# Retention followed by a low-rank mixer and MLP: loads in the order of need, positional decay, tiled low-rank steps, and the next batch's retention woven by hand into the MLP

## The chip, the cores and the metric

One core of one Trainium2 chip. The metric is the time of one execution on the device, in microseconds (us), lower is better. A run more than 1.5% above the fastest of the same kernel is called slow, and slow runs are left out of every comparison. The granted clock is the share of its full rate at which TensorE may run, by the profile's record, as a mean over the run.

Words used throughout: "up" is the first matmul of the MLP and "down" the second; a "tile" or "piece" is one sum in one bank of PSUM, TensorE's output memory; to "evict" is to copy a sum out of its bank, after which the bank is free; qd and kd are q and k with the decay multiplied in, vb is v cast to bfloat16.

Engines in the profile: PE is TensorE's matmuls, PEld its weight loads, DVE is VectorE, ACT is ScalarE, POOL is GpSimd, SP is SyncE, which issues loads and stores.

## The reference

Batch 4, 8 heads, 768 tokens, head size 64, model width 512. First a retention with a decay for each head, then a mixer over tokens of rank 32, then an MLP of width 2048 over channels:

```python
gamma = 1.0 - 2.0 ** (-5.0 - np.arange(H))            # per head
for t in range(S):
    state = gamma * state + outer(k[t], v[t])         # per batch and head, 64 x 64
    y[t]  = scale * q[t] @ state
x  = y as (batch, tokens, heads*head_dim)             # 768 x 512
h  = x.T @ U @ V                                      # U 768 x 32, V 32 x 768
u  = x + h.T
out = u + relu(u @ w_ch1) @ w_ch2                     # 512 -> 2048 -> 512
```

Inputs and output are float32; both kernels multiply in bfloat16.

## The kernel before

Tokens go in six chunks of 128. Retention of a chunk is done with matmuls: scores of the chunk against itself under a mask that holds the decay, plus the query times the state carried from the chunk before.

```python
def retnet_chunk(b, ci, x_sb, state_sb):
    # three loads of 256 KB: q_n, k_n, v_n (ring of three buffers each)
    nc.gpsimd.tensor_tensor(qd, q_n, Gq, op=ALU.mult)     # decay by place in the chunk
    nc.gpsimd.tensor_tensor(kd, k_n, Gk, op=ALU.mult)
    nc.scalar.activation(vb, v_n, AF.Copy)
    # ... 8 matmuls against the identity: qT_p, kT_p; two ACT evictions
    # ... 8 score matmuls with 64 rows; two DVE multiplies by maskA, maskB
    # ... o_p = a @ vb (+ qT @ state); one ACT eviction into x_sb[:, ci]
    for p in range(4):
        nc.tensor.matmul(st_p[:, ts(p, P)], kd[:, ds(2 * p, 2)], vb[:, ds(2 * p, 2)],
                         start=True, stop=first)
        if not first:                                     # the old state, decayed by gI
            nc.tensor.matmul(st_p[:, ts(p, P)], gI[:, ts(p, P)], state_sb[:, ts(p, P)],
                             start=False, stop=True)
    nc.vector.tensor_tensor(ns, st_p, bmask, op=ALU.mult)
```

The mixer of a batch is a list of tasks: a projection with 32 stationary columns, eight pieces of uT, 32 up pieces, six down tiles. Sums take turns in two PSUM banks, 6 and 7:

```python
def t_proj():
    for j in range(NCK):                                  # 6 matmuls of 512 columns
        nc.tensor.matmul(p_p, Ub[:, j], x_sb[:, j], ...)
def t_uT(c, lo, sz, idx):
    nc.tensor.matmul(piece, P_sb[:, ts(c, P)], Vb[:, ds(lo, sz)], ...)    # 32 rows
    # ... plus x transposed through the identity; evicted by ACT or DVE in turn
def t_mlp1(m, lo, sz):
    g_p = bank(6 + m % 2, free=sz)                        # 4 matmuls, then ReLU
def t_mlp2(j):
    nc.tensor.matmul(ch_p, Vb[:, ds(j * P, P)], P_sb, start=True, stop=False)
    # ... 16 matmuls of 512 columns; DVE adds x; store
```

The order of the whole:

```python
retnet(0)
retnet(1)
setup_weights()                                           # 8.4 MB, on ScalarE's queue
interleave(mixer_tasks(0, xs[0]), 2)                      # mixing of 0 with retention of 2
interleave(mixer_tasks(1, xs[1]), 3)
for t in mixer_tasks(2, xs[2]): t()
for t in mixer_tasks(3, xs[3]): t()
```

A scheduler at build time fixes the order of instructions on each engine. Each engine has its own list: in the run a_uv_late below, a ScalarE instruction that waited 5.00 us for its load held up the one behind it, which needed nothing from it.

## Time and profile before

| | kernel before |
|---|---|
| timed, two runs | 323.53 and 330.51 us |
| profiled span | 321.5 us |
| first low-rank matmul of batches 0 to 3 (PE timeline) | 75.2, 137.8, 200.2, 260.0 us |
| first up matmul of batches 0 to 3 | 84.2, 147.9, 210.3, 267.5 us |

The page of the profile, kernel before: the span cut into 40 slices of 8 us. Digits are tenths of busy time; PEclk is the granted TensorE clock in tenths; GB/s is what the DMA engines moved.

```profile
span 321.5 us, 4612 instructions
...
PE   0246845768999999999999999899999988999995
...
PEclk9999975555999999999999999759999995999999
DMA  7999999999994533154000011000001110000111
GB/s 240 251 291 261 258 245 308 213 277 217 159 189 100 129 99 99 65 148 82 2 2 2 35 65 65 35 0 0 0 2 65 65 67 0 0 0 2 65 65 65
```

PE is full or nearly so (8 or 9) from the tenth slice to the last but one, and DMA before that. There are two lower stretches of PEclk after the start, near 205 to 215 us and at 265 us. The table of stretches of the kernel before, cut where the mixing of a batch begins (start:end, length, busy time of each engine with its instructions, then clock, DMA share and GB/s):

```profile
core 0: us, PE busy (x) PEld busy (x) DVE busy (x) ACT busy (x) POOL busy (x), PEclk, DMA share, GB/s
0.00:75.20 75.20, 39.05 (x400) 29.34 (x400) 39.18 (x80) 35.40 (x68) 34.35 (x32) 0.80 1.13 258
75.20:137.80 62.60, 61.61 (x443) 32.38 (x448) 24.91 (x43) 21.99 (x43) 15.18 (x12) 0.97 0.59 127
137.80:200.20 62.40, 61.50 (x465) 33.00 (x469) 26.06 (x45) 21.61 (x43) 12.52 (x10) 1.00 0.19 51
200.20:260.00 59.80, 56.39 (x287) 26.12 (x290) 16.89 (x29) 11.48 (x23) 0.00 (x0) 0.91 0.07 27
260.00:321.50 61.50, 54.22 (x265) 25.07 (x268) 16.67 (x28) 9.80 (x20) 0.00 (x0) 0.94 0.08 30
```

The first 75 us move 258 GB/s. (The DMA share adds up the time of packets and can pass 1.) Each later line is one batch of mixing; the first two hold the retention of another batch as well. The last two do not, but for one last chunk, yet are only 1 to 3 us shorter: they also have the lower clock.

The chain of work that ended last, kernel before, over the loading stretch (start, length, what):

```profile
0.74 6.18 DMA q_n<-in_q_dram
...
17.00 10.44 DMA k_n<-in_k_dram
...
34.44 7.57 DMA k_n<-in_k_dram
...
42.84 14.58 DMA q_n<-in_q_dram x2
...
62.52 6.86 DMA st<-in_moe_w_ch_dram
...
75.28 2.69 PE bk_71_942 L228 x6
```

The chain goes from load to load, and reaches the first mixing matmul at 75.28 us. Last, the PE timeline of the kernel before, where batch 2 does its up pieces of 256 columns (start, length, line, output, operands):

```profile
229.50 0.60 PE L259 MATMUL bk_263_2608<-uT_2435,w1b 128*128 128x256 bf16 x4
229.93 0.60 PE L259 MATMUL bk_264_2614<-uT_2435,w1b 128*128 128x256 bf16 x4
230.61 0.60 PE L259 MATMUL bk_265_2620<-uT_2435,w1b 128*128 128x256 bf16 x4
```

The starts are 0.43 and 0.68 us apart in turn, so 1.1 us a pair. Four matmuls of 256 columns would be 0.43 us, by the 0.216 us measured for one of 512: every second piece waits for one of two banks to be evicted.

### The profile page before, as it was taken

To read this page: it belongs to the slowest core of one execution; us is meant where nothing else is said; L and a number is where in the kernel's file an instruction comes from. 1 tells how busy PE (TensorE), PEld (TensorE's weight loads), DVE (VectorE), ACT (ScalarE), POOL (GpSimd) and SP (SyncE) were. 2 spreads that over 40 slices of the span, in tenths; PEclk is the share of its full clock that TensorE was granted. 3 is DMA by queue.
4 is the path that set the end of the run, shared out by engine and by line. 5 is a ranking of instruction groups with operands and counts; after the bars stand their busy time and mean duration, and the time that the engine had idled before them with its cause. 6 is when DMAs were issued, how large, how long until landed. Compare 5 with 4: busy or idle time off the path is not lost.

```text
span 321.5 us, 4612 instructions
## 1 busy us (share of the span) xinstructions
PE 272.8 (85%) x1852; PEld 145.9 (45%) x1872; DVE 123.7 (38%) x222; ACT 100.3 (31%) x197; POOL 62.0 (19%) x54
## 2 busy tenths in 40 slices
PE   0246845768999999999999999899999988999995
PEld 0135734544546744455467444334554433455441
DVE  4864534354555531155456121424322122342111
ACT  2436653643655510055454000313310011322000
POOL 0556552637314310063041000000000000000000
PEclk9999975555999999999999999759999995999999
DMA  7999999999994533154000011000001110000111
GB/s 240 251 291 261 258 245 308 213 277 217 159 189 100 129 99 99 65 148 82 2 2 2 35 65 65 35 0 0 0 2 65 65 67 0 0 0 2 65 65 65
DMA packets 83412, 34.04 MB, mean 106 GB/s; under 512 B 76192, under 2 KB 76192, under 8 KB 83392
## 3 DMA queue, kind: packets, MB, share of 16 engines
q1 hardware_dynamic: 79168, 25.37, 36.5%
q10 hardware_dynamic: 4224, 8.39, 7.6%
q8 instruction: 14, 0.23, 0.3%
q14 instruction: 6, 0.05, 0.1%
HBM read 27.46 MB, written 6.29 MB: 105 GB/s over the span
## 4 chain that ended last, share of the span: by engine, by line
PE 71%; DMA 14%; DVE 5%; issue 4%; POOL 3%; ACT 1%; SPq 1%; POOLq 0%; DVEq 0%
DMA q_n<-in_q_dram 6%; DMA k_n<-in_k_dram 6%; DMA st<-in_moe_w_ch_dram 2%; POOL kd L165 2%; POOL qd L164 2%; DVE gT_2436 L265 1%; DVE gT_2813 L265 1%; PE bk_328_3168 L278 1%; PE bk_327_3147 L278 1%; PE bk_325_3105 L278 1%; PE bk_324_3084 L278 1%; PE bk_281_2791 L278 1%; PE bk_278_2728 L278 1%; PE bk_277_2707 L278 1%; PE bk_228_2339 L278 1%
## 5 line engine op out<-in xcount | busy, mean ns | idle before, releaser
L259 PEld LDWEIGHTS <-w1b 128*128 128x128 bf16 x512 | 49.6, 100 | 41.4 <-issue 15.0
L164 POOL TENSOR_TENSOR qd<-q_n,Gq 128x512 bf16<-128x512 f32 x24 | 31.4, 1307 | 87.2 <-PE bk_149_1646 L173 24.3
L165 POOL TENSOR_TENSOR kd<-k_n,Gk 128x512 bf16<-128x512 f32 x24 | 30.8, 1285 | 20.7 <-DMA k_n<-in_k_dram 8.1
L171 PEld LDWEIGHTS <-qd 128*128 128x128 bf16 x96 | 9.3, 116 | 19.9 <-POOL qd L164 16.1
L166 ACT ACTIVATE vb<-v_n 128x512 bf16<-128x512 f32 x24 | 15.0, 627 | 9.6 <-DMA v_n<-in_v_dram 5.1
L278 PEld LDWEIGHTS <-gT_2436 128*128 128x128 bf16 x96 | 8.9, 98 | 11.3 <-issue 1.4
L278 PEld LDWEIGHTS <-gT_940 128*128 128x128 bf16 x96 | 8.9, 98 | 11.2 <-issue 1.4
L278 PEld LDWEIGHTS <-gT_1688 128*128 128x128 bf16 x96 | 8.9, 98 | 11.2 <-issue 1.4
L278 PEld LDWEIGHTS <-gT_2813 128*128 128x128 bf16 x96 | 8.9, 98 | 11.3 <-issue 1.4
L173 PEld LDWEIGHTS <-kd 128*128 128x128 bf16 x96 | 8.7, 113 | 11.0 <-POOL kd L165 9.6
L198 PEld LDWEIGHTS <-aA 128*128 128x128 bf16 x96 | 10.3, 110 | 6.8 <-DVE aA L191 5.8
L198 PEld LDWEIGHTS <-aB 128*128 128x128 bf16 x96 | 10.6, 114 | 4.2 <-DVE aB L192 3.5
L171 PE MATMUL bk_1_176<-ident,qd 128*128 128x128 bf16 x4 | 0.8, 308 | 13.2 <-POOL qd L164 13.2
L210 PEld LDWEIGHTS <-kd 128*128 128x128 bf16 x80 | 9.0, 118 | 4.0 <-issue 3.8
L187 PEld LDWEIGHTS <-kT 64*128 64x128 bf16 x192 | 7.7, 108 | 6.2 <-ACT kT L178 3.2
L213 PEld LDWEIGHTS <-gI 128*128 128x128 bf16 x64 | 7.5, 119 | 4.7 <-issue 4.2
L202 PEld LDWEIGHTS <-qT 128*128 128x128 bf16 x80 | 8.8, 110 | 0.3
L244 ACT ACTIVATE uT_2812<-bk_283_2823 128x512 bf16<-128x512 f32 x1 | 0.6, 597 | 26.4 <-PE bk_283_2823 L241 26.4
L177 ACT ACTIVATE qT<-bk_230_2393 128x512 bf16<-128x512 f32 x1 | 0.6, 597 | 22.5 <-PE bk_231_2394 L173 22.5
L177 ACT ACTIVATE qT<-bk_148_1645 128x512 bf16<-128x512 f32 x1 | 0.6, 597 | 22.0 <-PE bk_149_1646 L173 22.0
L275 PEld LDWEIGHTS <-Vb 32*128 32x128 bf16 x24 | 2.2, 91 | 9.2 <-issue 8.9
L132 ACT ACTIVATE w1b<-st 128x2048 bf16<-128x2048 f32 x2 | 3.8, 1906 | 4.0 <-DMA st<-in_moe_w_ch_dram 4.0
(801 smaller groups left out, 593.2 us busy)
## 6 DMA issues: line engine op xcount, KB each, us to landing
st<-in_moe_w_ch_dram ACTq DMA_DIRECT2D x8, 1024.0 KB, 6.7
q_n<-in_q_dram SPq DMA_DIRECT2D x24, 256.0 KB, 5.1
k_n<-in_k_dram SPq DMA_DIRECT2D x24, 256.0 KB, 4.9
v_n<-in_v_dram SPq DMA_DIRECT2D x24, 256.0 KB, 4.9
out_dram<-o_sb SPq DMA_DIRECT2D x24, 256.0 KB, 2.0
Uf<-in_moe_U_dram SPq DMA_DIRECT2D x1, 96.0 KB, 7.1
Vf<-in_moe_V_dram SPq DMA_DIRECT2D x1, 96.0 KB, 6.4
```

The source lines that it names most:

```text
L164: nc.gpsimd.tensor_tensor(qd, q_n, Gq, op=ALU.mult)
L165: nc.gpsimd.tensor_tensor(kd, k_n, Gk, op=ALU.mult)
L166: nc.scalar.activation(vb, v_n, AF.Copy)
L171: nc.tensor.matmul(qT_p[:, ts(p, P)], qd[:, ds(2 * p, 2)], ident, start=True, stop=True)
L173: nc.tensor.matmul(kT_p[:, ts(p, P)], kd[:, ds(2 * p, 2)], ident, start=True, stop=True)
L187: nc.tensor.matmul(sp[:, ts(h // 2, P)], hsl(kT, h), hsl(qT, h), start=True, stop=True)
L198: nc.tensor.matmul(o_p[:, ts(h, D)], a[:, ts(h // 2, P)], vb[:, h], start=(h % 2 == 0), stop=(first and h % 2 == 1))
L202: nc.tensor.matmul(o_p[:, ts(p, P)], qT[:, ts(p, P)], state_sb[:, ts(p, P)], start=False, stop=True)
L210: nc.tensor.matmul(st_p[:, ts(p, P)], kd[:, ds(2 * p, 2)], vb[:, ds(2 * p, 2)], start=True, stop=first)
L213: nc.tensor.matmul(st_p[:, ts(p, P)], gI[:, ts(p, P)], state_sb[:, ts(p, P)], start=False, stop=True)
L259: nc.tensor.matmul(g_p, w1b[:, c, ts(m, P)], uT_sb[:, c, ds(lo, sz)], start=(c == 0), stop=(c == NCB - 1))
L278: nc.tensor.matmul(ch_p, gT_sb[:, m, ds(j * P, P)], w2b[:, m], start=False, stop=(m == NM - 1))
```

## The change

The intent is to start the MLP sooner and to give PE less to do and fewer waits. The kernel is rewritten; its core, shortened and in places paraphrased:

```diff
-    rin: q_n, k_n, v_n, three buffers each; weights through their own staging on ScalarE's queue
+    RING = 30                        # one FIFO of 256 KB loads on one queue, in the order of use:
+    for ci in range(NCK): feed_chunk(0, ci)          # batch 0
+    ... w1 (16 loads), w2 (16 loads) ...
+    for b in range(1, B): ...                        # batches 1 to 3
@@ decay by place in the whole sequence: the state needs no decay of its own
-        nc.gpsimd.tensor_tensor(qd, q_n, Gq, op=ALU.mult)
+        nc.gpsimd.tensor_tensor(qd, q_n, gq[:, ci, :, None].to_broadcast([P, H, D]), op=ALU.mult)
-            nc.tensor.matmul(st_p[...], gI[...], state_sb[...], start=False, stop=True)
+            # st_p stays in its bank; each chunk adds to it
@@ q and k transposed into one bf16 bank, evicted at once by DVE
-        nc.scalar.activation(qT, qT_p, AF.Copy); nc.scalar.activation(kT, kT_p, AF.Copy)
+        nc.vector.tensor_copy(out=qkT, in_=tp.rearrange("p (n m) -> p n m", n=8))
@@ low rank in tiles of the array
-                nc.tensor.matmul(p_p, Ub[:, j], x_sb[:, j], ...)                   # 512 columns
+                nc.tensor.matmul(p_p[ds(RK * c, RK), :P], Ub[:, j], x_sb[:, j, ts(c, P)], ...)
+                nc.tensor.matmul(banks[c - c0][...], V4[ds(RK * c, RK), ts(j, P)], pc[ds(RK * c, RK)], ...)
+        # u = x + low rank is formed (DVE), kept, and transposed for the MLP
@@ MLP
-                g_p = bank(6 + m % 2, free=sz)
+                g_p = bank("mlp", bufs=3)
-                nc.tensor.matmul(ch_p, Vb[:, ds(j * P, P)], P_sb, start=True, stop=False)
-                nc.vector.tensor_tensor(o_sb, ch_p, x_sb[:, j], op=ALU.add)
+                nc.vector.tensor_tensor(o_sb, ch, u[:, j], op=ALU.add)
@@ order by hand on PE, GpSimd and SyncE
-    retnet(0); retnet(1); setup_weights(); interleave(...)
+    with tc.manual_schedule(engines={ENG.PE, ENG.Pool, ENG.SP}):
+        load_uv()
+        for s in retnet_steps(0): s()
+        ... casts of w1 and w2 ...
+        for b in range(1, B):
+            if b == 1:
+                for s in lowrank_steps(0): s()
+            weave(mlp_pieces(b - 1), retnet_steps(b) + lowrank_steps(b),
+                  0.5 if b == 1 else 0.02, 0.97)
+        for _, f in mlp_pieces(B - 1): f()
```

The steps of retention are turn(c) (transposes and state), score(c) and mix(c), issued as turn(c+1), score(c), mix(c). ScalarE and VectorE are still ordered by the scheduler. One thing more changes: of three up pieces ScalarE now evicts two and VectorE one, where they took turns before.

## The prediction

> **What bounds it now.** The profiled span is 321.5 us (timed 323.5 to 330.5). In the PE timeline, mixing of batch 0 starts at 75.2 us, of 1 at 137.8, of 2 at 200.2, of 3 at 260.0. Two regimes:
>
> - 0 to 75 us: loading. The DMA row stands near 9 at 258 GB/s, and the chain of waits runs through q_n, k_n and weight loads: retention of two batches (9.4 MB) and all weights (8.4 MB) come before the first mixing. PE's clock is half from 50 to 80 us, and before 37 us 128-column matmuls also start 107 ns apart.
> - 75 to 321 us: PE, 88 to 98% busy. Four 512-column matmuls start 0.86 us apart (216 ns each); the Trainium skill ("TensorE: Matmul & The Clock Gate", Back-to-back issue gap) gives 512/2.4 + 2.5, the same. Counting columns, one batch of mixing is 110,592 (46 us), one of retention 19,456 (8 us). Batches 0 and 1 take 62.5 us each against 54; 2 and 3 about 60 against 46: two dips to half clock (205 to 215 and near 265 us, in the sparse low-rank stretch) and the two-bank wait of the 256-column up matmuls (1.1 us a pair, not 0.87).
>
> **Costing.**
>
> 1. Loads in need order: only batch 0 (4.7 MB) stands before the weights. In the trace, stretches with q/k/v alone move about 220 GB/s, weights about 330. Estimate: batch 0 landed at 26 us, w1 at 40, w2 at 53. Retention of batch 0 ends at 37; its low-rank part is a bare chain (projection, four expands on two banks, three turns on one) at 0.69 us per 512-column DVE eviction, about 1.2 for 1,024: 11 us. First up matmul at 48 us, not 84. Retention of batch 1 moves into batch 0's MLP; its PE time returns there.
> 2. PE columns: no Vb matmul in down (-3,072), column-tiled projection (-2,300 if four tiles run together), row-tiled expand (-1,500), no gI matmuls (-2,048): mixing 103,700, retention 17,408. About 15 us in all.
> 3. Three MLP banks: about 3 us a batch.
> 4. Low-rank steps spread between MLP pieces: the dips go, 8 to 10 us.
> 5. Given back: DVE takes per chunk the qkT eviction (1.2), state and two masks (2.1), then expand adds and turns: about 30 us a batch. For batch 1, woven into half an MLP, DVE is near full and each mix waits for masks issued one 0.75 us step earlier: 6 to 8 us of stalls. Batches 2 and 3 have 1.5 us per step: 2 to 3 each. The Trainium skill ("TensorEngine Tiling (Array Packing)", PSUM Bottleneck) warns that tiling speeds TensorE, not eviction.
>
> **Sum.** 48 + 2.5 (cold clock at MLP start) + 4 x 41.8 (MLP) + 3 x 7.7 (retention) + 3 x 3 (low rank) + 12 (stalls) + 3.7 (tail) = 265. Some 35 of the saving come from the earlier start.
>
> **Predicted: 264 us, 248 to 286.** Faster by over 2%: 0.96; within: 0.02; slower: 0.02.
>
> **Right or wrong by.** First up matmul at 44 to 54 us; up pieces 0.87 and 0.44 us apart; down tile 3.5; no clock dip after 55 us; batch-to-batch 52 to 56 us; DVE 75% and more from 70 to 100 us; four projection tiles per 55 to 60 ns.
>
> **What would make it wrong.** Casts, ordered on ACT and DVE by a scheduler I don't see, could hold batch 0's evictions until w2 lands (+5 to 15). The clock may dip in the weaves (+5 to 15). Tiled matmuls may serialise (+2 to 6). A shorter low-rank chain or fewer stalls would give 250.

## The result, and the profile after

The changed kernel ran in 275.54 and 275.89 us (median 275.72; before 323.53 and 330.51). The ratio is 0.8524, with a 95% interval of 0.8486 to 0.8562. A ratio here is the mean time of one kernel's fast runs over that of the other's fast runs of the same rounds, so not quite the ratio of the medians quoted.

The same rows of the page, changed kernel (slices of 6.8 us):

```profile
span 273.8 us, 4712 instructions
...
PE   0275754799988989978999999999999999999994
...
PEclk9999999999999999999999999999999999999999
DMA  8999999999999999200920211100001111000211
GB/s 155 214 218 226 300 387 383 264 223 218 210 221 219 217 234 248 61 0 38 208 62 4 77 41 77 41 0 2 0 2 62 56 77 38 2 0 0 79 77 77
```

PE is full or nearly so from about 52 us, not 75. No slice shows a lower clock. The first slices must be read with care: the record of the clock holds no entry before 55.4 us, and the row then shows 9 although the matmuls start 107 ns apart for 128 columns, which is half of 2.4 GHz. The Trainium skill ("TensorE: Matmul & The Clock Gate", What's actually happening) names half clock as the idle state, and the spacing agrees. Go by spacing where a row could be a default.

The table of stretches, changed kernel, cut at the first up matmul of each batch and at the last matmul:

```profile
core 0: us, PE busy (x) PEld busy (x) DVE busy (x) ACT busy (x) POOL busy (x), PEclk, DMA share, GB/s
0.00:52.00 52.00, 24.91 (x257) 18.15 (x258) 24.81 (x57) 15.04 (x27) 14.14 (x21) 1.00 1.13 271
52.00:113.90 61.90, 57.84 (x482) 31.73 (x481) 33.55 (x55) 22.53 (x44) 18.96 (x18) 1.00 1.10 210
113.90:172.80 58.90, 55.39 (x482) 31.25 (x481) 30.10 (x51) 17.65 (x35) 12.25 (x12) 1.00 0.22 63
172.80:228.10 55.30, 54.42 (x482) 31.02 (x481) 29.60 (x50) 16.28 (x32) 6.13 (x6) 1.00 0.08 30
228.10:269.80 41.70, 41.67 (x225) 21.80 (x223) 9.72 (x16) 10.67 (x22) 0.00 (x0) 1.00 0.10 39
```

The prediction's sum can be set beside these five lines and the tail:

| term | predicted us | measured us |
|---|---|---|
| first up matmul | 48 | 52.0 |
| batch 0's MLP with batch 1's retention and low rank (2.5 + 41.8 + 7.7 + 3 + 7 of stalls) | 62 | 61.9 |
| batch 1's, with batch 2 (41.8 + 7.7 + 3 + 2.5) | 55 | 58.9 |
| batch 2's, with batch 3 | 55 | 55.3 |
| batch 3's MLP | 41.8 | 41.7 |
| tail | 3.7 | 4.0 |
| sum: span | 265.5 | 273.8 |
| timed less span | not counted | 1.9 |

Two terms hold nearly all of the miss: the start (4.0) and batch 1 (3.9). The up pieces of 256 columns, PE timeline of the changed kernel:

```profile
242.34 0.60 PE L319 MATMUL mlp_2993<-uT_2717,w1b 128*128 128x256 bf16 x4
242.77 0.60 PE L319 MATMUL mlp_2999<-uT_2717,w1b 128*128 128x256 bf16 x4
```

They are 0.43 us apart and no longer come in uneven pairs. In the last batch a down tile takes 3.45 us (16 matmuls).

Where the start goes: the chain of work that ended last, changed kernel, in one chunk of batch 0's retention.

```profile
18.30 0.60 ACT x_183 L240
18.90 0.53 ACT vb_2_269 L179
...
19.46 0.60 PE st_207 L201 x4
...
20.09 0.60 DVE state_2_294 L207
...
20.70 0.68 DVE a_0_1_297 L225
21.38 0.61 DVE a_0_1_299 L225
...
22.03 0.24 PE o_310 L233
...
23.05 0.02 ACT x_183 L240
...
23.54 0.63 ACT vb_3_326 L179
```

This is a loop. The eviction of x comes first on ACT, then the cast of the v after next, then the state matmul, the state on DVE, the two masks, the mix, and the eviction of x again. It takes 4.75 us a chunk (from 18.30 to the next x at 23.05), while the loads of a chunk come every 3.6 us. By the trace (issue of each part's last load, plus its time to landing) batch 0 is in by 27.1 us, w1 by 40.3 and w2 by 51.7, near the predicted 26, 40 and 53; retention still ends at 39.9 us, where the prediction had 37. The low-rank chain after it takes 12.1 us, where it had 11. So of the 4.0 us of the start 2.9 are retention and 1.1 the chain.

Where batch 1 loses: the timeline of all engines, changed kernel, when its up stage begins.

```profile
113.92 1.03 PE L319 MATMUL mlp_1459<-uT_1320,w1b 128*128 128x512 bf16 x4
...
117.34 1.02 PE L319 MATMUL mlp_1502<-uT_1320,w1b 128*128 128x512 bf16 x4 [0.69 <-ACT gT_1458 L326]
...
120.85 1.02 PE L319 MATMUL mlp_1543<-uT_1320,w1b 128*128 128x512 bf16 x4 [0.69 <-ACT gT_1458 L326]
...
124.23 0.68 DVE L347 TENSOR_TENSOR o_4_1397<-mlp_1348,u_613 128x512 f32<-128x512 f32 x1
...
128.77 0.68 DVE L347 TENSOR_TENSOR o_5_1455<-mlp_1418,u_613 128x512 f32<-128x512 f32 x1
```

Up pieces of 512 columns start 1.7 to 1.8 us apart in place of 0.86. After every second one 0.7 us goes to a step of retention; the others wait for the eviction of the piece just before them (0.69 us), as if there were one bank and not three. The last two lines say why: the additions of batch 0's output tiles 4 and 5 come at 124.2 and 128.8 us, though their sums were complete near 108 and 114 us, and each holds a bank of the three until then. VectorE shows no idle time just before either addition, and stood idle for 1.7 to 2.4 us four times from 110 to 122 us: the additions were not kept from it by its load, but came late in its list.

### The profile page after: what moved, and what is told of

It reads as the page before. It is cut to its first block, busy times and chain, and to the rows that moved or that the text cites. A ratio compares the mean times of both kernels' runs of the same rounds, so it can differ in the third digit from the quotient of the medians.

```text
span 273.8 us, 4712 instructions
## 1 busy us (share of the span) xinstructions
PE 234.2 (86%) x1920; PEld 134.0 (49%) x1920; DVE 128.5 (47%) x230; ACT 82.2 (30%) x159; POOL 51.5 (19%) x57
## 4 chain that ended last, share of the span: by engine, by line
PE 75%; DVE 12%; issue 4%; ACT 3%; DMA 3%; ACTq 1%; POOL 1%; DVEq 0%; POOLq 0%
DMA Vf<-in_moe_V_dram 2%; DVE u_613 L284 2%; PE mlp_2001 L342 1%; PE mlp_2711 L342 1%; PE mlp_1905 L342 1%; PE mlp_2820 L342 1%; PE mlp_2110 L342 1%; PE mlp_2615 L342 1%; PE mlp_3183 L342 1%; PE mlp_3143 L342 1%; PE mlp_3083 L342 1%; PE mlp_3163 L342 1%; PE mlp_3123 L342 1%; PE mlp_3103 L342 1%; PE mlp_2772 L342 1%
## 5 line engine op out<-in xcount | busy, mean ns | idle before, releaser
L342 PEld LDWEIGHTS <-gT_2890 128*128 128x128 bf16 x96 | 9.4, 98 | 11.1
L342 PEld LDWEIGHTS <-gT_2180 128*128 128x128 bf16 x96 | 8.6, 98 | 9.0
L342 PEld LDWEIGHTS <-gT_1458 128*128 128x128 bf16 x96 | 8.6, 98 | 9.0
L342 PEld LDWEIGHTS <-gT_712 128*128 128x128 bf16 x96 | 8.0, 98 | 7.0
L188 PE MATMUL qk_196<-ident,qd_0_184 128*128 128x128 bf16 x4 | 0.6, 308 | 11.5 <-POOL qd_0_184 L175 11.5
L279 PEld LDWEIGHTS <-V_80 32*128 32x128 bf16 x96 | 3.6, 97 | 12.0 <-issue 12.0
L175 POOL TENSOR_TENSOR qd_0_911<-in_524,gq 128x512 bf16<-128x512 f32 x1 | 1.3, 1295 | 25.6 <-DMA in_524<-in_q_dram 25.6
L175 POOL TENSOR_TENSOR qd_3_2388<-in_1226,gq 128x512 bf16<-128x512 f32 x1 | 1.0, 1042 | 26.6 <-PE qk_2194 L188 26.6
L188 PEld LDWEIGHTS <-qd_0_184 128*128 128x128 bf16 x4 | 0.3, 130 | 11.5 <-POOL qd_0_184 L175 11.5
L300 ACT ACTIVATE uT_2717<-qk_2850 128x1024 bf16<-128x1024 bf16 x1 | 1.0, 1023 | 14.0 <-PE qk_2850 L295 14.0
L300 ACT ACTIVATE uT_2007<-qk_2140 128x1024 bf16<-128x1024 bf16 x1 | 1.0, 1023 | 13.5 <-PE qk_2140 L295 13.5
L175 POOL TENSOR_TENSOR qd_3_1678<-in_605,gq 128x512 bf16<-128x512 f32 x1 | 1.0, 1042 | 17.5 <-PE qk_1478 L188 17.5
L342 PE MATMUL mlp_1348<-w2b,gT_712 128*128 128x512 bf16 x16 | 4.1, 382 | 0.0
L342 PE MATMUL mlp_1243<-w2b,gT_712 128*128 128x512 bf16 x16 | 4.1, 380 | 0.0
L342 PE MATMUL mlp_1038<-w2b,gT_712 128*128 128x512 bf16 x16 | 4.1, 380 | 0.0
L342 PE MATMUL mlp_905<-w2b,gT_712 128*128 128x512 bf16 x16 | 4.1, 380 | 0.0
L342 PE MATMUL mlp_1143<-w2b,gT_712 128*128 128x512 bf16 x16 | 4.1, 380 | 0.0
L342 PE MATMUL mlp_2001<-w2b,gT_1458 128*128 128x512 bf16 x16 | 4.0, 380 | 0.0
L342 PE MATMUL mlp_2062<-w2b,gT_1458 128*128 128x512 bf16 x16 | 4.0, 380 | 0.0
L342 PE MATMUL mlp_2711<-w2b,gT_2180 128*128 128x512 bf16 x16 | 4.0, 380 | 0.0
```

The lines of the kernel that those rows point to most:

```text
L175: nc.gpsimd.tensor_tensor(qd, q_n, gq[:, ci, :, None].to_broadcast([P, H, D]), op=ALU.mult)
L188: nc.tensor.transpose(tp[:, ts(p, P)], qd[:, ds(2 * p, 2)], ident)
L279: nc.tensor.matmul(banks[c - c0][:, ts(j - j0, P)], V4[ds(RK * c, RK), ts(j, P)], pc[ds(RK * c, RK)], start=True, stop=True)
L300: nc.scalar.activation(dst, src, AF.Copy)
L342: nc.tensor.matmul(ch, gT[:, m, ts(j, P)], w2b[:, m], start=(m == 0), stop=(m == NM - 1))
```

## The experiments

Twelve runs; all gave correct results. All were timed in rounds beside the kernel before except one look. In the four calls (the result's own and three of experiments) the fast runs of the kernel before average between 323.5 and 324.5 us, so differences of about 1 us between kernels of different calls are not read from the times alone. The median leaves out the slow run of b_need_order. "Changed" is 275.7 us.

| run | what | us, median | ratio to before | first up matmul, us |
|---|---|---|---|---|
| b_need_order | before, with the new batch order | 310.1 | 0.9576 | 59.4 (from b_need_order_2) |
| a_two_first | changed, with the old batch order | 283.6 | 0.8755 | 79.1 |
| a_two_banks | changed, two MLP banks | 283.8 | 0.8762 | 52.1 |
| a_bare_lowrank | changed, low rank not woven | 296.4 | 0.9152 | 52.7 |
| a_out6 | changed, six output buffers | 272.0 | 0.8387 | 52.3 |
| a_uv_late | changed, casts of U and V later | 275.3 | 0.8480 | 52.7 |
| a_first_qd | the same, first cast of v off ScalarE | 274.4 | 0.8460 | 50.4 |
| a_deep | changed, retention one step deeper | 263.2 | 0.8115 | 46.5 |
| a_hi_late | changed, part of low rank later | 272.7 | 0.8402 | 49.0 |
| a_best | a_deep, a_hi_late and a_out6 together | 261.5 | 0.8063 | 44.2 |
| a_best30 | a_best, weave from 0.3 | 260.3 | 0.8036 | 43.4 |

### Where the gain comes from: one part alone, three parts undone

Theory: the order of loads is the main source. Rival: the columns, banks and weaving are.

**b_need_order**, the kernel before with one edit:

```diff
-    retnet(0); retnet(1); setup_weights()
-    interleave(mixer_tasks(0, xs[0]), 2); interleave(mixer_tasks(1, xs[1]), 3); mixer 2; mixer 3
+    retnet(0); setup_weights()
+    interleave(mixer_tasks(0, xs[0]), 1); interleave(mixer_tasks(1, xs[1]), 2)
+    interleave(mixer_tasks(2, xs[2]), 3); mixer 3
```

> The kernel before with one thing changed: retention of batch 1 is no longer done ahead of the weights, but interleaved with mixing of batch 0 (2 with 1, 3 with 2). Theory 1 (order of loads and of batches is the main source of the gain): first mixing at 45 to 52 us in place of 75, less some 10 us for retention that is now done later, so a span near 305 us (298 to 310). Rival (the gain is in columns, banks and weaving; the order only moves work about): within 2% of before, 315 us or more.

Three fast runs: 309.21, 310.13 and 311.01 us, 4.2% less than before, some 14 us; their spans, 307.4 to 309.2 us, lie in the theory's range for the span, and the times below the rival's. The fourth run, the profiled one, took 446 us: its record grants a clock of 0.5 to 0.65 from 37 us to the end. Nothing is read from it.

**b_need_order_2**, the same kernel, one look for a usable profile:

> The same kernel as b_need_order, for a profile in the fast state (the first one fell at a granted clock of 0.60). Fast runs gave 309 to 311 us. Expected: first mixing at 45 to 52 us in place of 75.2, batch 0's step longer than 62.5 us by 0 to 3, batch 2's step near 62 in place of 59.8, so that of 25 us of earlier start some 14 are left.

310.89 us, one run, within the range of the fast ones. The projection begins at 39.3 us (45 to 52 was expected), the first up matmul comes at 59.4 in place of 84.2, so 25 us earlier. From projection to projection the batches then take 78, 63 and 63 us. Of 25 us, 14 are left at the end, as expected. The expected step of batch 0 was wrong (78, not 62 to 65): its projection is issued as chunks of x come, and the up stage begins 20 us after it.

**a_two_first**, the changed kernel with the order undone:

```diff
-    for ci in range(NCK): feed_chunk(0, ci)
+    for b in range(2):
+        for ci in range(NCK): feed_chunk(b, ci)
     ... weights ...
-    for b in range(1, B): ...
+    for b in range(2, B): ...
-        for s in retnet_steps(0): s()
+        for s in retnet_steps(0): s()
+        for s in retnet_steps(1): s()
-            rs = retnet_steps(b)
+            rs = retnet_steps(b) if b > 1 else []
```

> The changed kernel with that order undone: loads and retention of batches 0 and 1 both come before the weights and the first mixing. Theory 1: first up matmul near 80 us in place of 52 (a second latency-bound retention of 29 us, and 21 us of loads), batch 0's MLP shorter by 12 to 15 us since no retention is woven into it, so 289 to 294 us, 13 to 18 above the changed kernel. Rival: 275 to 280 us.

283.58 us, 7.9 more than changed; less than expected and more than the rival. The first up matmul comes 27.1 us later (79.1), but batch 0's MLP is 15.3 us shorter (46.6 us, since it carries no retention), and batch 1's 3.6 us shorter (55.3, like batch 2's: the late additions are gone). So a first matmul that is 27 us earlier is worth 8 us in this kernel: what was taken out of the start comes back inside the MLP. The 8 are a low figure: 3.6 us of what the undoing costs are hidden by the late additions going; without them it would be about 11.5, by subtraction, which no run tested.

**a_two_banks**: `bank("mlp", bufs=3)` becomes `bufs=2`.

> The changed kernel with two banks in place of three for the MLP's sums. Theory (the prediction: third bank worth about 3 us a batch): 10 to 14 us more than the changed kernel, 286 to 290 us; up pieces of 256 columns back to 1.1 us a pair. More, up to 20, if late output additions hold both banks. Rival (evictions keep up with two): under 3 us.

283.78 us, 8.1 more, so about 2 us a batch on average where the prediction had 3. Both the theory and the rival were off; the theory by less. In batch 3, where nothing is woven in, the up stage takes 23.3 us in place of 20.9, with pieces of 256 columns about 1.1 us a pair, as in the theory. The average hides a spread: by the first up matmuls the four batches take 3.9, −0.4, 2.1 and 2.3 us more. Batch 1 takes no more because its third bank is of little use in the changed kernel, where late additions hold two of the three. VectorE's order changes with the edit too (those additions come at 117.0 and 120.6 us here), so this run isn't the bank alone.

**a_bare_lowrank**:

```diff
-            weave(mlp_pieces(b - 1), rs + ls, 0.5 if b == 1 else 0.02, 0.97)
+            weave(mlp_pieces(b - 1), rs, 0.5 if b == 1 else 0.02, 0.97)
+            for s in ls: s()
```

> The changed kernel with the eight low-rank steps of batches 1 to 3 done in one piece after the MLP of the batch before, not woven into it; retention stays woven. Theory: each bare chain costs 8 to 10 us in place of about 3 of matmuls, and the clock may drop to half for 7 to 10 us after it as in the kernel before: 12 to 30 us more than the changed kernel. Rival (weaving low rank hides little): under 6 us, and no dip of the clock.

296.37 us, 20.7 more: the largest single part found. The clock row of its page, and the beginning and end of one bare chain in its PE timeline, with the first up pieces after it:

```profile
PEclk9999999999999995799999995899999985999999
```

```profile
107.98 0.52 PE L266 MATMUL o<-x,Ub 128*32 128x128 bf16 x24
...
117.89 1.01 PE L295 MATMUL qk<-ident,u 128*128 128x128 bf16 x8 [1.11 <-ACT uT L300]
...
119.55 1.06 PE L319 MATMUL mlp<-uT,w1b 128*128 128x512 bf16 x2 [0.22 <-issue]
```

The chain takes 10.7 us (107.98 to 118.69) for some 3 us of matmuls at full clock. In the record the clock is at half from 111.7 to 121.9 us, and so twice more, 10.2 us each. The last two lines show it: eight transposes of 128 columns take 1.01 us (0.61 at full clock, in the changed kernel), and the two up matmuls last 1.06 us where two take 0.59 at full clock. No wait of PE within the chain is over 1.11 us; in the 3.7 us from the chain's start to the drop PE was busy for 1.5. So low rank done in one piece costs its own latency and a clock drop that goes on into the MLP. The three undone parts add to 36.7 of the 48 us; the fewer matmul columns (15 us by count) were not undone by themselves, and parts need not add.

### Where the prediction lost 11 us

**a_out6**: `tc.tile_pool(name="outp", bufs=3)` becomes `bufs=6`.

> The changed kernel with six output buffers in place of three. In the changed kernel's trace the up stage of batch 1 starts its first 512-column pieces 1.7 us apart until 129 us, because the additions of output tiles 4 and 5 of batch 0 come at 124.2 and 128.8 us in the vector engine's order, though their sums were complete near 108 and 114, and hold two of the three banks; this order follows from output buffers that are given back late (the stores of tiles 0 and 1 are issued 10 us after they are ready, behind loads in the same queue). Theory: with six buffers the additions come at once, up of batch 1 takes 28 us in place of 31, as in batch 2, and the whole 3 to 5 us less: 271 to 273 us. Rival (the vector engine is simply full there, whatever the order): within 1 us of 275.7.

272.03 us, 3.7 less, as the theory had it. The two additions, VectorE timeline of this run:

```profile
107.86 0.69 DVE L347 TENSOR_TENSOR o<-mlp,u 128x512 f32<-128x512 f32 x1 [0.18 <-PE mlp L342]
...
113.95 0.69 DVE L347 TENSOR_TENSOR o<-mlp,u 128x512 f32<-128x512 f32 x1 [1.03 <-PE mlp L342]
```

They come 16 and 15 us earlier, each as soon as its sum is there. Batch 1's up stage takes 27.7 us in place of 31.2. With three buffers the fifth addition could not have a buffer before the store of tile 1, which sits in the SyncE list behind loads (issued at 99.3 us, ready at 89.8). But in the changed kernel's trace that store had landed 4.8 us after its issue, near 104 us, before the fifth sum was complete, and the store of tile 2 (issued at 103.8, landed 4.1 us later) before the sixth. So what held these additions in the run was their place in VectorE's list and not a buffer. The edit made the scheduler choose another order; that it had reckoned with late buffers is the likely reason, but isn't shown.

**a_uv_late**:

```diff
-        load_uv()                                 # with both casts on GpSimd at once
-        for s in retnet_steps(0): s()
+        uv_casts = load_uv()                      # loads only
+        for i, s in enumerate(retnet_steps(0)):
+            if i == 13: uv_casts()
+            s()
```

> The changed kernel with the two GpSimd casts of U and V moved from ahead of the first chunk to just ahead of the sixth. The first qd comes at 10.4 us since GpSimd waits for V until 9.3. Theory (retention of batch 0 is a chain of latencies, 4.75 us a chunk, that starts with the first qd): first qd at 5.5 to 6.5 us, first up matmul at 47.5 to 48.5 in place of 52.0, 271 to 272 us in all. Rival (the loads of batch 0 set the end of that retention): first up above 50.5, less than 1.5 us gained.

275.32 us: nothing gained, and the first qd came at 10.73 us, later than before the edit (10.42). The timeline of this run shows a second thing that had stood at the same place:

```profile
9.67 0.63 ACT L181 ACTIVATE vb<-in 128x512 bf16<-128x512 f32 x1 [5.00 <-DMA in<-in_v_dram]
10.20 0.23 ACT L142 ACTIVATE gq<-pos 128x48 f32<-128x48 f32 x1
...
10.73 1.04 POOL L177 TENSOR_TENSOR qd<-in,gq 128x512 bf16<-128x512 f32 x1 [9.43 <-DVE gq L144]
```

GpSimd waits for gq, the decay, and ScalarE computes gq only after the cast of the first v, which waits for its load until 9.67 us. An order on ScalarE that no data requires held the first step. This run could not test the theory, since it did not bring about the earlier qd.

**a_first_qd**: a_uv_late, and for the first chunk of batch 0 the cast of v is done by GpSimd:

```diff
-            nc.scalar.activation(vb, v_n, AF.Copy)
+            if b == 0 and ci == 0: nc.gpsimd.tensor_copy(out=vb, in_=v_n)
+            else: nc.scalar.activation(vb, v_n, AF.Copy)
```

> Second try at the start. In a_uv_late the first qd did not come earlier (10.7 us), since the cast of the first v, which waits for its load until 9.7, stands ahead of the two exponentials of the decay in ScalarE's order. Here that one cast is done on GpSimd after the first kd, so the exponentials are first on ScalarE. Theory: gq is ready near 6 us, first qd at 5.5 to 6.5, second turn near 12 in place of 13.9, and with the chunk period of 4.75 us unchanged the first up matmul 1.5 to 2.5 us earlier, total 273 to 274.3. Rival (the loads alone pace batch 0): total within 0.7 of 275.5.

274.38 us. Now the first qd is at 5.25 us, but the second waits for its load until 10.52, and the first up matmul comes 1.6 us earlier (50.4). So of 5 us at the first step 1.6 are left; the loads hold the second chunk. The first up matmul is as the theory had it; the time is 0.1 above its range. It is 0.9 us under a_uv_late: too little to be read from the times. It was run at another time.

**a_deep**:

```diff
-        for ci in range(NCK + 1):      # turn(ci), score(ci - 1), mix(ci - 1)
+        for ci in range(NCK + 2):      # turn(ci), score(ci - 1), mix(ci - 2)
-    rmid = ctx.enter_context(tc.tile_pool(name="rmid", bufs=3))
+    rmid = ctx.enter_context(tc.tile_pool(name="rmid", bufs=4))
```

> The changed kernel with retention pipelined one step deeper: mix of chunk c comes after turn of c+2 and score of c+1, and there are four buffers in place of three. The wait of each mix for its two masks (1.0 and 0.36 us a chunk in batch 0, 0.5 to 0.9 in batch 1) should go. Theory (these waits are on the critical path, as the prediction has it with 6 to 8 us for batch 1): chunk period of batch 0 from 4.75 to about 3.6 us, first up 5 to 7 us earlier, batch 0's MLP 3 to 5 us shorter, in all 8 to 12 us less: 264 to 268 us. Rival (the vector engine's load, or the cast of v behind the x copy, sets the pace): under 3 us.

263.24 us, 12.5 less: slightly more than expected, and the largest gain of a single edit. The casts of v of chunks 2, 3 and 4 of batch 0, ScalarE timeline of this run:

```profile
16.38 0.63 ACT L179 ACTIVATE vb<-in 128x512 bf16<-128x512 f32 x1 [2.98 <-DMA in<-in_v_dram]
...
20.00 0.63 ACT L179 ACTIVATE vb<-in 128x512 bf16<-128x512 f32 x1 [0.61 <-DMA in<-in_v_dram]
...
23.67 0.63 ACT L179 ACTIVATE vb<-in 128x512 bf16<-128x512 f32 x1 [1.09 <-DMA in<-in_v_dram]
```

The period is 3.6 to 3.7 us, and each cast now waits for its load; in the changed kernel these casts stood behind the eviction of x, 4.75 us apart (18.79, 23.54 and 28.29 us in its ScalarE timeline). The first up matmul comes at 46.5 (5.5 earlier), batch 0's step takes 57.6 us in place of 61.9, batch 1's 56.6 in place of 58.9. VectorE does the same work as before the edit (22.8 us in the woven half of batch 0's step in both), so its load was not the bound. PE's recorded waits for the masks of batch 1's mixes, 2.8 us in all in the changed kernel, no longer appear. Some 2 us of the gain are in batch 1's step, where the additions come less late (the sixth 13 us after the first up matmul, not 15; the fifth 3 us after it, not 10).

The edit changes two things at once, and the list of ScalarE with it: three casts of v, not two, now stand ahead of the first eviction of x. So the expected rival's second half, the cast of v behind the x copy, is not ruled out: this edit removes it too. How much each contributes was not separated. A third suspect is the clock, since the record grants full clock from 18.7 to 28.9 us here. But a_best30 below, with the same retention steps for batch 0, has full clock for 3.4 us only (from 19.3) and begins its projection at the same 34.7 us (39.9 in the changed kernel), so the clock is not where the earlier start comes from.

**a_hi_late**:

```diff
-                for s in lowrank_steps(0): s()
+                lr = lowrank_steps(0)
+                for i in (0, 1, 2, 5, 6): lr[i]()          # what tokens 0 to 511 need
...
+            if b == 1:
+                for at, i in ((2, 3), (5, 4), (8, 7)): pieces.insert(at, (0.0, lr[i]))
```

> The changed kernel with the part of batch 0's low rank that only tokens 512 to 767 need (two expands, the third turn) moved behind the first up pieces, which read tokens 0 to 511 alone. Theory (the bare chain of 12 us before the first up matmul is all on the critical path): first up near 47 to 48 us in place of 52, total 271 to 272.5 us. Rival (what was moved stalls the first pieces as much): under 1.5 us.

272.72 us, 3.0 less, first up at 49.0: just short of the expected 47 to 48 and 272.5, and far from the rival.

**a_best** is a_deep, a_hi_late and a_out6 in one, **a_best30** the same with `0.3 if b == 1` in place of 0.5:

> The changed kernel with the three edits together that each gained when run alone: retention one step deeper, six output buffers, the late part of batch 0's low rank behind the first up pieces. If the gains add: first up near 43.5 us, 263.2 less 3.0 (low rank) less 1 to 2.5 (late additions; the deeper pipeline already shortens up of batch 1 from 31.2 to 29.1 us), so 257.5 to 259.5 us. If they overlap: 261 or more.

> The same with the weaving of batch 1 into batch 0's MLP started at 0.3 of it in place of 0.5. Theory (with half an MLP for 26 steps some steps still wait for the one before, and a longer stretch gives them room): 2 to 4 us less than a_best. Rival (loads of batch 1, which land in order after the weights, are not there yet at 0.3; chunk 0 lands near 60 us): 0 to 3 us more.

261.47 and 260.34 us. The gains overlap: 12.5, 3.0 and 3.7 give 14.2 together. In both a_deep and a_best the clock record changes to full at 49.4 us, though a_best's first up matmul is 2.3 us earlier: its first pieces run at half clock, so a start that is moved forward is partly paid back. At the first up matmul of batch 1 a_best is even 0.6 us behind (104.7 against 104.1): on top of a_deep, the later low rank gained nothing. Batch 1's step is 1.1 us shorter (55.5 against 56.6), which fits the output buffers. The earlier weave gives another 1.1 us (the ranges, 260.0 to 261.3 and 261.0 to 262.5 us, just overlap), less than its theory's 2 to 4. a_best30 is the fastest kernel here: 0.8036 of before (0.8001 to 0.8070), and 5.6% less than the changed kernel.

## Why the prediction was right or wrong

- **The total.** 275.7 lies within 248 to 286 and 12 us above the 264. The mechanism was right: the start shrinks from load-bound 84 us to about 50, then PE is bound. Its sum, built batch by batch from columns and measured spacings, matched the two batches without an unforeseen wait within 0.3 us, and batch 0 within 0.1. Part of that closeness is luck: in batch 2's step the profile counts PE busy for 54.4 of 55.3 us, so 0.9 of idle time in place of 2.5 of stalls, and 1.9 more of work than the 52.5 predicted. In batch 0's step the idle time is 4.1, not 7.
- **"Retention of batch 0 ends at 37 ... First up matmul at 48 us": mis-sized.** It came at 52.0. The loads landed about as predicted (3.6 us a chunk). The prediction's 37 leaves out that retention goes round a loop through ScalarE, PE and VectorE (4.75 us a chunk), which set the pace; this cost 2.9 us, and the low-rank chain another 1.1. a_deep breaks the loop and gets the first up matmul to 46.5.
- **"Batches 2 and 3 have 1.5 us per step: 2 to 3 each" of stalls: mis-sized for batch 2's weave.** That step of 58.9 us had 6.4 of stalls, by the prediction's own figures for its work. The 3.9 us above the estimate are two banks held by late additions; in a_out6 the same step takes 55.4. The prediction counted banks but not who gives them back, nor when that engine's list comes to it.
- **"For batch 1 ... DVE is near full ... 6 to 8 us of stalls": right in size, wrong in reason.** The step was 61.9 of 62 predicted. But VectorE was busy 17.4 of the 30 us from 70 to 100, 58% and not 75%. The 1,024-element eviction of qkT took 0.69 us, not 1.2: it is in bfloat16. The Trainium skill states this ("VectorE: DVE Perf Modes", Why PSUM operands drop a tier: a PSUM operand allows twice the rate at most, and the single rate for fp32), and the trace agrees: 0.69 us for 1,024 in bf16 and 0.69 for 512 in fp32. The stall is latency and order: a_deep, at the same VectorE load, shortens this step by 4.3 us.
- **Clock: right.** No dip from 55.4 us to the end. a_bare_lowrank shows that the weave is what removes the dips, with three of 10.2 us when it is taken out. The item "8 to 10 us" counted the dips alone: taking the weave away in the changed kernel costs 20.7, the latency of the bare chain included. These are not the same quantity, so the item is neither shown right nor wrong.
- **"Some 35 of the saving come from the earlier start": wrong as a net figure.** The start is 32 us earlier, but undoing the order alone costs 7.9 us in the changed kernel, and doing it alone gains 14 in the old one. The prediction said itself that the work returns; the sum accounts for it, the sentence does not.
- **Banks: about 3 us a batch predicted, 2.0 measured on average** (3.9, −0.4, 2.1 and 2.3). Pieces are 0.863 and 0.437 us apart, the down tile takes 3.45 us, as said.
- **Projection tiles: slower than said.** 24 tiled matmuls take a slot of 0.45 us (0.075 us for four, not 0.055 to 0.060), still a third of the 1.3 us that six matmuls of 512 columns need. The warning that tiling does not speed eviction fits: each 512-column eviction after the tiled expands still takes 0.69 us.
- **Batch-to-batch 52 to 56 us: right for one of three** (61.9, 58.9, 55.3); the line contradicted the prediction's own sum for the first.
- **Timed less span**, 1.9 us, was left out of the sum.

## What to carry to other kernels

Sum a new schedule stage by stage from measured spacings, and find what a part is worth by undoing it: an earlier start is worth only what does not come back later, here 8 of 27 us (more without the late additions). Where engines pass a chunk round a loop, the loop's latency and not the load rate may set the pace; one more step of pipelining between a product and its mask, with the casts that it let ScalarE do earlier, gained 12.5 us here, the most of any single edit tried on the changed kernel. When a stage runs as if it had fewer banks than it has, look for the late reader that holds them, and then at the order of that reader's engine: here the buffer was free, and the list was late.

## What the Trainium skill lacked or had wrong

- "TensorE: Matmul & The Clock Gate" (Why this matters for your kernels) says to have no PE-idle gaps over about 3 us. In a_bare_lowrank the longest PE wait in the low-rank chain is 1.11 us, yet the clock drops to half 3.7 us after the first chain begins, with PE busy for 1.5 of these 3.7 us, and stays there for 10.2 us; so in all three chains (the drop comes after 3.7, 3.7 and 5.6 us). Gaps under 3 us were not enough here. The page tells of frequent short idles in one other kernel, but names no busy share below which the clock falls; three chains don't give one either.
- The same page says that the clock's ratio is binary, 4/8 or 8/8, apart from 13/16 when three cores of a die are busy. The slow run of b_need_order (446 us, a one-core program) records 0.56 and 0.65 for most of its length, and its 512-column matmuls start 402 and 360 ns apart there (216 at full clock). What other cores of the chip did then is not known.
- The same page, on reading the clock: the record can have no entry at the start (none before 55.4 us in the changed kernel), and a profile may then show full clock where 128-column matmuls start 107 ns apart. The page does warn that the record can be unreliable and has a check by the total of throttled time; a missing start, and the spacing as the check for it, it does not name.
- "VectorE: DVE Perf Modes" held (0.69 us for 1,024 bf16 elements out of PSUM) and lacked nothing that was needed here. The same 128 x 1,024 bf16 eviction takes 1.02 us on ScalarE.
- None of the pages looked up gives the effect of a broadcast operand on GpSimd: the multiply of 128 x 512 took a median 1.27 us with a full table (kernel before) and 1.04 with the decay broadcast along 64 elements (changed kernel). Nothing else was held equal, and spans on GpSimd are rough in this profile.
